# A Fourier-mixing and Hardswish kernel on one core: which batches the first four chunks of a pair take, and when the second batch is loaded

## The chip, the cores and the metric

The kernel runs on one core of a Trainium2 chip. The metric is device time in microseconds (us) of one execution. Before the change, three executions took 1940.53, 1941.27 and 1941.79 us: the median is 1941.27 us.

## What is computed

```python
x: (8, 3008, 256)                                  # 8 batches, float32
X = np.fft.fft(np.fft.fft(x, axis=1), axis=2).real # Fourier mixing, real part
h = X.reshape(24064, 256) @ w_in                   # 256 -> 2048
g = h * np.clip(h + 3.0, 0.0, 6.0) / 6.0           # Hardswish
out = g @ w_out                                    # 2048 -> 256
```

## The kernel before

The sequence length is 3008 = 47 x 64: a row number is n1 * 64 + n2 with n1 below 47 (`N1`) and n2 below 64 (`N2`). The transform over the sequence is done as a 47-point stage (**stage1**) and a 64-point stage (**stage2**), and symmetries of a real input are used: n2 is folded onto 32 values, and so is the last axis.

The eight batches are worked through as four **pairs** of two batches. For a pair, x comes in as 8 pieces of four n2 values each (`NXC` pieces of `XC`). For each piece there is a straight load (`load_forward`) and a gather of the mirrored rows (`load_partners`, an indirect DMA whose row numbers are in `IX`). `fold` adds and subtracts the two (L187 to L201, 5 vector operations a piece, a few more for the last one), stage1 multiplies the result by a table of 47-point sines and cosines, the results are copied to SBUF (tile `z`) and written to a scratch area in DRAM (`zd`). From there `load_g` reads them back in another order, a **group** `gr` of four k1 values at a time for both batches (six groups), stage2 multiplies them by the tables `T`, and the result is the tile `q` that the dense part uses. One row of it is spread over all partitions as `qn` (`spread`, through DRAM; `spread_by_pe` does the same with matmuls).

The dense part takes 12 **chunks** of a pair (`ck`), two from each group, and each chunk in 8 **steps** (`fc`, one step for 256 of the 2048 columns of the hidden layer), so 96 steps a pair and 384 in all; step s below counts from the first one of the program. In a step TensorE makes the two first products u and v (`mlp1_products`, L394), VectorE and ScalarE make the Hardswish of them (`activate`: L403, L413, L415, L440, L443), GpSimd makes sums of the results (`combine`, L457), and TensorE multiplies by seven prepared mixtures of w_out blocks (`mlp2`, L487; in the first chunk the plain blocks, `mlp2_first`, L467). The program is written out by hand: the order on each engine's queue is the order of the source. `mlp1` runs two steps ahead of `mlp2`. Work for later groups and the next pair is put beside given steps by `beside`, ahead of the step's own work or (`at=behind`) after its `mlp1`. When a chunk has ended, `store` transposes its results and sends them out, 8 DMAs of 32 KB from SP's queue in the second step of the next chunk and 8 in the third; `finish` (GpSimd) comes before them in the first.

Before step 0 there is a **prologue**. For the first pair it does not use `stage1` but `stage1_first` (L253): both batches lie side by side on 94 partitions, one table `F0` holds both, and a product is one matmul over the whole. Eight times, in `ORDER` (the last piece first), the prologue loads a piece on GpSimd's queue, folds it on VectorE and makes its stage1. Three pieces are asked for ahead, since their tiles are three. The parts of `zd` that group 0 needs are written at once, the rest by DMAs kept in the list `later`, which steps 1 and 3 issue. Then follow `load_g` of group 0, half of its stage2, and `u` and `v` of steps 0 and 1; the second half of group 0's stage2 stands between these two.

Beside this the weights are prepared (their values are taken apart into exponent and mantissa and put together again): `load_w` brings 16 pieces of 512 KB; `exponent_a` (ScalarE, L604), `exponent_b` (TensorE, L621), `exponent_c` (ScalarE, L624), `mantissa` (VectorE, L632, L633) and `join` (VectorE, L641, L647) treat one; and for w_in `fold_w_in` multiplies it by the cosine table (L673), copies it to `W1` (L675) and moves one row of it into the columns `WN` (L679, SP's queue), which L403 needs. `load_w(0)` to `load_w(3)` are issued late in the prologue, `load_w(4)` to `(7)` once group 0 has arrived (`see`), the others in steps 0 and 1. The calls in steps 0 to 7 are in `first_steps` and `second_steps`. `mix_w_out` (GpSimd, four operations) makes the mixtures for `mlp2`: twice in step 5, and in steps 8 and 9.

Of the kernel before, what the change touches and what calls it, by code (L numbers as in the profile page):

```python
# [58 lines left out]
def kernel(  # L59
# [21 lines left out]
    PR0, PZ0 = 2 * N1, 2 * PZ  # L81
    XC = 4
    NS = N2 // 2
    NXC = NS // XC
    KC = 4
# [29 lines left out]
    F = consts.tile([P, 5 * PB], F32, name="F")  # L115
    F0 = apool.tile([PR0 + 2, 6 * PZ0], F32, tag="a", name="F0")
# [10 lines left out]
    class Pair:  # L127
        def __init__(self, p):
            self.p = p
            self.x, self.xr, self.y, self.z = {}, {}, {}, {}  # L130
            self.zd = self.zq = None
            self.g, self.q, self.qn = {}, {}, {}

    ORDER = [NXC - 1] + list(range(NXC - 1))

    def x_tile(pr, c):
        pool, tag = (spool, "t") if pr.p == 0 and ORDER.index(c) % 3 == 2 else (xpool, "x")
        return pool.tile([PX, XC, D], F32, tag=tag, name="xt")  # L140
# [8 lines left out]
    def load_forward(pr, c):  # L149
        xt = x_tile(pr, c)  # L150
        n = XC if c < NXC - 1 else XC - 1
        if pr.p == 0:
            o = xt[0:PR0 + 2]
            nc.gpsimd.dma_start(out=o[:, 0:n, :], in_=x_pn[0:PR0 + 2, c * XC + 1:c * XC + 1 + n, :])
            if n < XC:
                nc.gpsimd.dma_start(out=o[:, n:XC, :], in_=x_pn[0:PR0 + 2, 0:1, :])
        for b in range(2) if pr.p > 0 else ():
# [12 lines left out]
    def load_partners(pr, c):  # L170
        xr = x_tile(pr, c)
        pr.xr[c] = xr
        i = pr.p * NXC + c
        nr = PX if pr.p > 0 else PR0 + 2
        nc.gpsimd.indirect_dma_start(  # L175
            out=xr[0:nr].rearrange("p n d -> p (n d)"), out_offset=None, in_=x_r,
            in_offset=bass.IndirectOffsetOnAxis(ap=IX[0:nr, i:i + 1], axis=0),
        )

    def fold(pr, c, part, eng):  # L180
        nr = PX - 1 if pr.p > 0 else PR0
# [71 lines left out]
    def stage1_first(pr, c):  # L253
        y = pr.y.pop(c)
        n = XC if c < NXC - 1 else XC - 1

        def table0(i):
            return F0[0:PR0, i * PZ0:(i + 1) * PZ0]

        pt = ps_h.tile([P, 2 * TB], F32, tag="uv", name="pt")[0:PZ0]  # L260
        nc.tensor.matmul(pt[:, 0:n], table0(5), y[:, 0:n, P], start=True, stop=True)
        for k in range(2 if n < XC else 0):
            nc.tensor.matmul(pt[:, n:XC], table0(k + 1), y[:, n + k, P:P + 1], start=(k == 0), stop=(k == 1))

        k = ORDER.index(c)
        pool, tag = (zpool, "z") if k < 2 else (cpool, "c") if k < 5 else (qpool, "q") if k < 7 else (apool, "a")
        z = pool.tile([PZ0, XC, D + 1], F32, tag=tag, name="z")
        nc.scalar.copy(z[:, :, D], pt[:, 0:XC])
        for i in range(XC // 2):
            ps = bank([P, 2, D], "ps1")[0:PZ0]  # L270
            if (c, i) == (NXC - 1, XC // 2 - 1):
                nc.tensor.matmul(ps[:, 0], table0(0), y[:, 2 * i], start=True, stop=False, skip_group_check=True)
                for k, (j, cs) in enumerate([(XC - 1, slice(0, P + 1)), (XC, slice(0, P + 1)),
                                             (XC - 1, slice(P + 1, D)), (XC, slice(P + 1, D))]):
                    nc.tensor.matmul(ps[:, 1, cs], table0(k + 1), y[:, j, cs], start=False, stop=(k % 2 == 1),
                                     skip_group_check=True)
            else:
                nc.tensor.matmul(ps, table0(0), y[:, 2 * i:2 * i + 2, :], start=True, stop=True)
            nc.scalar.copy(z[:, 2 * i:2 * i + 2, 0:D], ps)
        if pr.zd is None:  # L280
            pr.zd = dpool.tile([NG, 2, 2 * KK, 2, NS, D + 1], F32, tag="zd0", name="zd")
        zd = pr.zd[:].rearrange("g b k c n d -> (g b k c) n d")[:, c * XC:(c + 1) * XC, :]

        n0 = PZ0 // NG
        nc.sync.dma_start(out=zd[0:n0], in_=z[0:n0])
        later.append((zd[n0:], z[n0:]))
# [18 lines left out]
    def load_g(pr, gr):  # L305
        g = gpool.tile([P, 2 * KK, D + 1], F32, tag="g", name="g")
        gb = [g[b * N2:(b + 1) * N2] for b in range(2)]
        for b in range(2):
            zd = pr.zd[b, gr] if pr.p > 0 else pr.zd[gr, b]
            zd = zd.rearrange("k c n d -> (c n) k d")  # L310
            if pr.p > 0 or gr > 0:
                nc.sync.dma_start(out=gb[b][:, :, 0:D if pr.p > 0 else D + 1], in_=zd)

        for h in range(2 if pr.p + gr == 0 else 0):
            ks = slice(h * KK, (h + 1) * KK)
            for b in range(2):

                (nc.sync if h + b == 0 else nc.gpsimd).dma_start(
                    out=gb[b][:, ks], in_=pr.zd[gr, b, ks].rearrange("k c n d -> (c n) k d"))
        for b in range(2) if pr.p > 0 else ():  # L320
            nc.sync.dma_start(out=gb[b][:, :, D], in_=pr.zq[gr, :, :, :, b].rearrange("k c n -> (c n) k"))
        pr.g[gr] = g

# [19 lines left out]
    def spread_by_pe(pr, gr, i, ps, copy=nc.scalar.copy):  # L343
        if i == 0:
            pr.qn[gr] = qpool.tile([P, 2 * TB], F32, tag="qn", name="qn")
        for u in range(2):
            kk = 2 * i + u
            nc.tensor.matmul(ps[:, u * P:(u + 1) * P], pr.g[gr][:, kk, D:D + 1].to_broadcast([P, P]),
                             T[:, :, gr, 1, kk], start=True, stop=True)
        copy(pr.qn[gr][:, i * TB:(i + 1) * TB], ps)  # L350
        if i == 1:
            del pr.g[gr]

    def spread(pr, gr):
        pr.qn[gr] = qpool.tile([P, 2 * TB], F32, tag="qn", name="qn")
# [6 lines left out]
    class Chunk:  # L362
# [3 lines left out]
        def __init__(self, pr, ck):  # L366
# [9 lines left out]
            self.blocks = [[(2 * (j % 2) + h, (k1[j], N1 - k1[j])[m]) for j in range(KC) for h in range(2)]  # L376
# [319 lines left out]
    nc.sync.dma_start(out=FI[:], in_=c_stage1[:, 5 * PB + 6 * PZ0:])  # L696
    nc.sync.dma_start(out=F0[:], in_=c_stage1[0:PR0 + 2, 5 * PB:5 * PB + 6 * PZ0])
# [35 lines left out]
    for c in ORDER[0:3]:  # L733
        load_x(first, c)
# [4 lines left out]
    for k, c in enumerate(ORDER):  # L739
        for part in range(2):  # L740
            fold(first, c, part, nc.vector)
        if k == NXC - 1:

            exponent_a(0)
        stage1_first(first, c)
        if k < NXC - 1:
            keep_awake(1)
        if k + 3 < NXC:
            load_x(first, ORDER[k + 3])
        else:  # L750
            for j in (2, 3) if k == 5 else ():
                load_w(j)
        if k == 4:
            load_w(0)
            load_w(1)
            load_t(0, slice(0, KK))
        elif k == 1:
            nc.sync.dma_start(out=C[:], in_=dim)
    load_g(first, 0)
    load_t(0, slice(KK, 2 * KK))  # L760

    seen = wpool.tile([P, 1], F32, tag="seen", name="seen")
    see(first.g[0][:, 0, 0:1])
# [23 lines left out]
    stage2(first, 0, 0)  # L787
    spread_by_pe(first, 0, 0, bank([P, TB], "ps3")[:])
# [7 lines left out]
    def beside(p):  # L796
# [7 lines left out]
        late = 4 if p == 0 else 0  # L804
        if p == 0:
            put(5, load_g, cur, 1)
            for gr in range(1, NG):
                put(gr + 1, load_t, gr)
            put(NF - 1, close_w)
            put(NF - 1, nc.sync.dma_start, F[:], c_stage1[:, 0:5 * PB])  # L810
# [6 lines left out]
        for gr in range(1, NG):  # L817
# [32 lines left out]
    stage2(first, 0, 1, copy=nc.vector.tensor_copy)  # L850
    spread_by_pe(first, 0, 1, spare[0][:, 0], copy=nc.vector.tensor_copy)
# [62 lines left out]
    for s, (p, ck, fc) in enumerate(steps):  # L914
# [4 lines left out]
        if s < NF:  # L919
# [6 lines left out]
            if s == 5:  # L926
                see(chunk(s + 1)[0].a[s + 1][:, 0, 0, 0:1])
                mix_w_out(0)
                mix_w_out(1)
        else:  # L930
# [6 lines left out]
            if s < NF + 2:  # L937
                mix_w_out(s - NF + 2)
# [11 lines left out]
def _tables(B, S, D):  # L950
# [19 lines left out]
    f1 = np.zeros((2, 64, 5, 64))  # L970
    f1[:, :N1, :, :2 * NK1] = f[:5].reshape(5, N1, -1).swapaxes(0, 1)

    f0 = np.zeros((128, 6, NK1 // 4, 2, 8))
    for b in range(2):
        f0[b * N1:(b + 1) * N1, :, :, b] = f.reshape(6, N1, NK1 // 4, 8).swapaxes(0, 1)

# [3 lines left out]
    for i in range(B):  # L980
        n = i % 2 * (64 if i > 1 else N1)
        row[n:n + N1, i // 2] = ((i * N1 + np.arange(N1)[::-1, None]) * 2 + 2) * npc - 1 - np.arange(npc)
    sign = 1.0 - 2.0 * (np.arange(128)[:, None] % 2)
    f = np.concatenate([f1.reshape(128, -1), f0.reshape(128, -1), row.reshape(128, -1), sign], axis=1)
# [45 lines left out]
```

## Time and profile before

| | |
|---|---|
| span of the profiled execution | 1938.6 us |
| median of the times | 1941.27 us, that is 2.7 us more than that span |
| busy share of the span | TensorE (PE) 99%, VectorE (DVE) 74%, ScalarE (ACT) 35%, GpSimd (POOL) 73% |
| granted TensorE clock | full in all 40 slices |
| first fold on VectorE starts | 7.88 us |
| first dense product (L394) starts | 43.60 us |
| first product with the mixtures (L487, step 8) starts | 110.87 us |
| DMA share in 0 to 25, 25 to 50, 50 to 75, 75 to 100 us | 0.87, 0.81, 0.68, 0.47 |

How to read it: the page gives one profiled execution, with busy times by engine, and then the chain of work that ended last. The trace behind it can be asked for the instructions of a stretch in order of time (the timeline), and for busy times in given stretches (the windows). A name like `u<-q,W` says what is written from what; L394 is the line of the program; SPq and POOLq are the queues on which SP and GpSimd issue DMAs, and a DMA's time there is that of its issue, not of its transfer. In a timeline row the first number is the start, the second the time from there to the end of the last instruction merged into the row, and `[0.52 <-DMA WN<-W]` tells how long the engine sat idle before it and what ended that. TensorE makes a float32 product in two passes, so one matmul of the program is counted as x2.

### The profile page before, as it was taken

Reading aid. Unit: us, or ns where it says so; the run is one execution under the profiler, and the core shown is the slowest. Engines: PE = TensorE matmul, PEld = TensorE weight load, DVE = VectorE, ACT = ScalarE, POOL = GpSimd, SP = SyncE. Lnnn points to the kernel's source line nnn. Section 1 sums busy time; section 2 is a strip of 40 time slices with the busy share of each in tenths; the row PEclk is TensorE's granted clock in tenths of the full one; section 3 lists DMA queues with packets and bytes.
Section 4 is the critical chain, followed back from the end, with each engine's and each line's share of the span. In section 5 each row is a group of like instructions: output and inputs, shape, how many; then the busy total and the mean of one; then the engine's idle time right before and its main releaser. Section 6 shows DMA issues by size and latency. Waiting matters only on the chain.

```text
span 1938.6 us, 27871 instructions
## 1 busy us (share of the span) xinstructions
PE 1922.3 (99%) x9220; PEld 1654.3 (85%) x9220; DVE 1438.2 (74%) x2780; ACT 679.9 (35%) x1161; POOL 1418.2 (73%) x1624
## 2 busy tenths in 40 slices
PE   9999999999999999999999999999999999999997
PEld 4688888888988888888898888888899888888887
DVE  7877777767777777777787777777778777777777
ACT  5634333333333333333333333333333333333332
POOL 4088888887678877787678877878666667666664
PEclk9999999999999999999999999999999999999999
DMA  8522221211112222121111221222110101101000
GB/s 248 177 60 63 59 53 50 55 46 33 35 34 58 67 56 55 44 52 33 34 36 49 53 55 44 52 53 50 35 28 20 28 17 28 34 11 28 21 18 20
DMA packets 149998, 96.57 MB, mean 50 GB/s; under 512 B 118991, under 2 KB 132307, under 8 KB 149854
## 3 DMA queue, kind: packets, MB, share of 16 engines
q1 hardware_dynamic: 138378, 57.57, 12.4%
q0 software_dynamic: 10816, 37.07, 6.7%
q8 instruction: 72, 1.18, 0.3%
q14 instruction: 72, 0.59, 0.1%
q10 hardware_dynamic: 660, 0.16, 0.0%
HBM read 57.44 MB, written 37.32 MB: 49 GB/s over the span
## 4 chain that ended last, share of the span: by engine, by line
PE 95%; DVE 2%; DMA 1%; issue 1%; ACT 1%; POOL 0%; SPq 0%; DVEq 0%; ACTq 0%; POOLq 0%
PE acc L487 56%; PE v L394 16%; PE u L394 16%; PE ps L337 2%; PE acc L467 1%; PE ps L223 1%; DVE a L443 1%; DMA xt<-in_x_dram,IX 1%; PE spare L673 1%; DVE s L403 0%; ACT t L440 0%; DVE o L548 0%; DVE u L424 0%; PE ex L621 0%; POOL xt L175 0%
## 5 line engine op out<-in xcount | busy, mean ns | idle before, releaser
L457 POOL TENSOR_TENSOR c<-a 128x512 f32<-128x512 f32 (+1 forms) x375 | 468.8, 1250 | 362.8 <-PE acc L487 312.4
L487 PE MATMUL acc<-c,G 128*128 128x256 f32 (+1 forms) x3008 | 696.9, 374 | 0.0
L440 ACT ACTIVATE t<-u,half 128x512 f32<-128x512 f32 (+1 forms) x384 | 260.6, 679 | 1141.9 <-DVE u L413 1058.9
L487 PEld LDWEIGHTS acc<-c,G 128*128 128x128 f32 x3008 | 565.4, 190 | 71.1
L403 DVE SCALAR_TENSOR_TENSOR s<-qn,WN,u 128x256 f32<-128x256 f32 (+1 forms) x768 | 330.6, 472 | 334.3 <-PE u L394 333.2
L487 PE MATMUL acc<-a,G 128*128 128x256 f32 (+1 forms) x2256 | 541.3, 375 | 0.0
L487 PEld LDWEIGHTS acc<-a,G 128*128 128x128 f32 x2256 | 421.5, 190 | 71.1 <-issue 17.5
L394 PE MATMUL v<-q,W 127*128 127x256 f32 (+1 forms) x1536 | 389.3, 375 | 3.0 <-DVE a L443 3.0
L394 PE MATMUL u<-q,W 128*128 128x256 f32 (+1 forms) x1536 | 388.0, 375 | 0.9 <-ACT q L340 0.9
L443 DVE SCALAR_TENSOR_TENSOR a<-t,u 128x512 f32<-128x512 f32 (+2 forms) x448 | 264.0, 601 | 102.3 <-ACT t L440 98.8
L394 PEld LDWEIGHTS v<-q,W 127*128 127x128 f32 x1536 | 287.8, 190 | 43.9 <-DVE a L443 3.6
L394 PEld LDWEIGHTS u<-q,W 128*128 128x128 f32 x1536 | 285.7, 190 | 37.6 <-issue 1.9
L457 POOL TENSOR_TENSOR c<-a,c 128x256 f32<-128x256 f32 (+1 forms) x375 | 268.6, 716 | 29.4
L457 POOL TENSOR_TENSOR c<-c,a 128x256 f32<-128x256 f32 (+1 forms) x375 | 268.5, 716 | 29.4
L413 DVE TENSOR_TENSOR u<-s,v 128x512 f32<-128x512 f32 x352 | 245.0, 696 | 36.7
L443 DVE SCALAR_TENSOR_TENSOR a<-t,v 128x512 f32<-128x512 f32 (+1 forms) x480 | 263.6, 566 | 0.3 <-ACT t L440 0.2
L440 ACT ACTIVATE t<-v,half 128x512 f32<-128x512 f32 (+1 forms) x384 | 260.5, 678 | 0.4 <-PE acc L487 0.2
L415 DVE TENSOR_TENSOR v<-v,s 128x512 f32<-128x512 f32 x352 | 243.9, 693 | 0.0
L457 POOL TENSOR_TENSOR r<-w,e 128x256 f32<-128x256 f32 (+1 forms) x92 | 88.7, 985 | 3.6
L497 ACT ACTIVATE e<-acc 128x512 f32<-128x512 f32 (+2 forms) x184 | 83.4, 544 | 0.0
L548 DVE STREAM_TRANSPOSE o<-r 128x256 f32<-128x256 f32 (+1 forms) x192 | 72.5, 415 | 0.2
L457 POOL TENSOR_TENSOR w<-w,e 128x512 f32<-128x512 f32 (+1 forms) x46 | 57.5, 1249 | 3.6
(110 smaller groups left out, 770.9 us busy)
## 6 DMA issues: line engine op xcount, KB each, us to landing
out_dram<-o SPq DMA_DIRECT2D x747, 32.0 KB
zd<-z SPq DMA_DIRECT2D x48, 192.0 KB
g<-zd SPq DMA_DIRECT2D x36, 256.0 KB
xt<-in_x_dram POOLq DMA_DIRECT2D x21, 256.0 KB
qn<-qd SPq DMA_DIRECT2D x19, 256.0 KB
st<-in_moe_w_in_dram POOLq DMA_DIRECT2D x8, 512.0 KB
st<-in_moe_w_out_dram POOLq DMA_DIRECT2D x8, 512.0 KB
xt<-in_x_dram POOLq DMA_DIRECT2D x17, 192.0 KB
```

What stands on the lines that cost most here:

```text
L223: nc.tensor.matmul(ps[b][h * PB:(h + 1) * PB, 0:n], F[rows(b), 0:PB], y[rows(b), 2 * h:2 * h + n], start=True, stop=not last, skip_group_c ...
L337: nc.tensor.matmul(ps[:, blk, u * P:n].rearrange("p (b k) -> p b k", b=2), g[:, kk, blk * (P + 1):blk * (P + 1) + P], T[:, :, gr, blk, kk, ...
L394: nc.tensor.matmul(ps[:, i, 0:nq], W1[r, blk, f * P:(f + 1) * P], q[r, blk, of:of + nq], start=True, stop=True)
L403: nc.vector.scalar_tensor_tensor(s[:, i, 0:nq], qn[:, of:of + nq], WN[:, f:f + 1], u[:, i, 0:nq], op0=AL.mult, op1=AL.add)
L413: nc.vector.tensor_tensor(u[:], s[:], v[:], op=AL.add)
L415: nc.vector.tensor_tensor(v[:], v[:], s[:], op=AL.subtract)
L440: nc.scalar.activation(t, h, AF.Relu, bias=half[:], scale=scale)
L443: nc.vector.scalar_tensor_tensor(dst, t, 1.0, h, op0=AL.min, op1=AL.mult)
L457: (eng or nc.gpsimd).tensor_tensor(out, in0, in1, op=AL.add)
L487: nc.tensor.matmul(ch.acc[i // 2][:, i % 2, 0:ch.n], G[:, i, fc, :], mv, start=(fc == 0 and i % 2 == 0), stop=(fc == NF - 1), skip_group_c ...
L497: nc.scalar.mul(ch.e[:, k:i + 1, 0:ch.n], ch.acc[i // 2][:, 0:i + 1 - k, 0:ch.n], 1.0 / WS)
L548: nc.vector.transpose(o[:, 0:n // DH, h], ch.r[:, m, h, 0:n].rearrange("p (j i) -> p j i", i=DH))
```

## The change

The first pair's first two groups are no longer made for both batches at once. Chunks 0 and 1 take 8 values of k1 from **batch 0**, chunks 2 and 3 the same values from **batch 1**; from chunk 4 on all is as before. So the prologue needs the x of batch 0 alone. A `Half` stands for one batch: its 8 pieces are taken as four double pieces m, piece m on partitions 0 to 46 and piece m + 4 on partitions 64 to 110 (`load_half`, `fold_half`, `stage1_half`), and the matmuls of the two halves use rows and columns 0 to 63 and 64 to 127 of TensorE. The tables `F0` are gone, `F` has a sixth table and is loaded at the start.

In the prologue the straight loads of batch 0 go on SP's queue, the gathers on GpSimd's; all four double pieces have tiles of their own, and `load_w(0)` to `(3)` come right behind them. Stage2 of group 0 is one call (`stage2_half`, two k1 values in the place of the second batch). The x of batch 1 is loaded in steps 2, 4, 4 and 5, folded on GpSimd in steps 3, 5, 6 and 7, and goes through `stage1_half` in steps 5, 7, 8 and 9. `mix_w_out` is moved to steps 4, 6, 9 and 11, and its `see` is dropped. Pair 1's loads start at step 12 and come every 8 steps (before: step 8, every 8). The diff, cut:

```diff
-    ORDER = [NXC - 1] + list(range(NXC - 1))
+    ORDER = [NM - 1] + list(range(NM - 1))
...
+    def load_half(hb, m, queue, pool=xpool, tag="x"):
+        hb.x[m], hb.xr[m] = x_tile(pool, tag), x_tile(pool, tag)
+        for h in range(2):
+            c = m + h * NM
+            nr = N1 + 1 if h else PB
+            n = XC if c < NXC - 1 else XC - 1
+            rows, o = x_pn[hb.b * N1:hb.b * N1 + nr], hb.x[m][h * PB:h * PB + nr]
+            queue.dma_start(out=o[:, 0:n, :], in_=rows[:, c * XC + 1:c * XC + 1 + n, :])
+            if n < XC:
+                queue.dma_start(out=o[:, n:XC, :], in_=rows[:, 0:1, :])
+        gather(hb.xr[m], hb.b * NM + m)
...
+    def stage1_half(hb, m):
+        y = hb.y.pop(m)
...
+        pt = ps_h.tile(...) if starting[0] else bank([P, 2 * TB], "pt")
+        for h in range(2):
...
+            nc.tensor.matmul(o[:, 0:n], table(5, h), y[rows(h), 0:n, P], start=True, stop=True)
...
+        nc.scalar.copy(z[:, :, D], pt[0:PX, 0:XC])
+        for i in range(XC // 2):
+            ps = bank([P, 2, D], "ps1") if starting[0] or i else ps_h.tile([P, 2, D], F32, tag="uv", name="ps1")
+            for h in range(2):
+                o = ps[h * PB:(h + 1) * PB]
...
+                nc.tensor.matmul(o[:, 0:n], table(0, h), y[rows(h), 2 * i:2 * i + n], start=True, stop=not end,
+                                 skip_group_check=True)
...
+            nc.scalar.copy(z[:, 2 * i:2 * i + 2, 0:D], ps[0:PX])
...
+        n0 = 2 * 4 * KK if hb.b == 0 else PZ
+        for h in range(2):
...
+            nc.sync.dma_start(out=dst[0:n0], in_=src[0:n0])
+            if n0 < PZ:
+                later.append((dst[n0:], src[n0:]))
...
+    def load_g_half(hb, gr, queue=nc.sync):
...
+        for t in range(2):
+            (queue if t else nc.sync).dma_start(out=g[t * N2:(t + 1) * N2, 0:KK], in_=zd[t])
...
+            if pr.p == 0 and ck < 4:
+                k1 = [ck % 2 * KC + j + 1 for j in range(KC)]
+                b = [ck // 2] * KC
...
-    for c in ORDER[0:3]:
-        load_x(first, c)
+    hb = halves[0]
+    for k, m in enumerate(ORDER):
+        load_half(hb, m, nc.sync, *((xpool, "x"), (xpool, "x"), (spool, "t"), (apool, "a"))[k])
+        if k == 0:
+            nc.sync.dma_start(out=F[:], in_=c_stage1[:, 0:6 * PB])
...
+    for j in range(4):
+        load_w(j)
+    nc.sync.dma_start(out=C[:], in_=dim)
+    load_t(0)
+    for k, m in enumerate(ORDER):
         for part in range(2):
-            fold(first, c, part, nc.vector)
+            fold_half(hb, m, part, nc.vector)
...
-        stage1_first(first, c)
+        stage1_half(hb, m)
...
-    stage2(first, 0, 0)
-    spread_by_pe(first, 0, 0, bank([P, TB], "ps3")[:])
+    stage2_half(hb, 0)
+    spread_by_pe(hb, 0, bank([P, TB], "ps3")[:])
...
+            put(3, load_g_half, halves[0], 1)
+            put(4, stage2_half, halves[0], 1)
+            put(5, spread_half, halves[0], 1)
...
+            hb = halves[1]
+            for k, m in enumerate(ORDER):
+                put((2, 4, 4, 5)[k], load_half, hb, m, nc.sync, *((qpool, "q") if k < 2 else (xpool, "x")))
+                for part in range(2):
+                    put((3, 5, 6, 7)[k], fold_half, hb, m, part, nc.gpsimd)
+                put((5, 7, 8, 9)[k], stage1_half, hb, m)
+            put(4, mix_w_out, 0)
+            put(6, mix_w_out, 1)
+            put(9, mix_w_out, 2)
+            put(11, mix_w_out, 3)
+            put(11, load_g_half, hb, 0)
+            put(11, load_g_half, hb, 1)
+            for gr in range(2):
+                put(12 + 4 * gr, stage2_half, hb, gr)
+                put(13 + 4 * gr, spread_half, hb, gr)
...
-                put(NST * (gr - 2) + 12, load_g, cur, gr)
-            s2(NST * (gr - 1) + (late if gr == 1 else 0), cur, gr)
+                put(NST * (gr - 2) + (12 if p > 0 or gr > 2 else 17), load_g, cur, gr)
+            s2(NST * (gr - 1), cur, gr)
...
-                t = 2 * late + (9 - late // 4) * c
+                t = 9 * c if p > 0 else 12 + 8 * c
...
-    stage2(first, 0, 1, copy=nc.vector.tensor_copy)
-    spread_by_pe(first, 0, 1, spare[0][:, 0], copy=nc.vector.tensor_copy)
```

More of the change, by code (lines that the diff above doesn't have):

```diff
@@ L149, in load_forward @@
     def load_forward(pr, c):
-        xt = x_tile(pr, c)
+        xt = x_tile()
         n = XC if c < NXC - 1 else XC - 1
[L152 to L157, printed above, removed]
+        for b in range(2):
             i = 2 * pr.p + b
@@ L308, in load_g @@
         for b in range(2):
[L309 to L319, printed above, removed]
+            zd = pr.zd[b, gr] if pr.p > 0 else pr.zd[b][gr]
+            nc.sync.dma_start(out=gb[b][:, :, 0:D if pr.p > 0 else D + 1], in_=zd.rearrange("k c n d -> (c n) k d"))
         for b in range(2) if pr.p > 0 else ():
@@ L695 @@
     keep_awake(9)
[L696 to L697 removed]
+    nc.sync.dma_start(out=FI[:], in_=c_stage1[:, 6 * PB:])
     bias = wpool.tile([P, 2], F32, tag="bias", name="bias")
@@ L968, in _tables @@
     f[2:5:2] = f[2:5:2, ::-1]
[L970 to L975, printed above, removed]
+    f1 = np.zeros((2, 64, 6, 64))
+    f1[:, :N1, :, :2 * NK1] = f.reshape(6, N1, -1).swapaxes(0, 1)
     npc = N2 // 8
```

193 lines of the change are left out of this document (111 added, 82 removed).

## The prediction

> **What bounds the kernel now.** I read the engines' busy times first, then the windows, then the timeline of the start, and last the places after step 8 that the change touches.
>
> ```profile
> PE 1922.3 (99%) x9220; PEld 1654.3 (85%) x9220; DVE 1438.2 (74%) x2780; ACT 679.9 (35%) x1161; POOL 1418.2 (73%) x1624
> ...
> 75.00:100.00 25.00, 25.00 (x88) 15.64 (x87) 20.47 (x39) 14.66 (x24) 3.06 (x6) 1.00 0.47 122
> ```
>
> TensorE (PE) is the bound. In the chain that ended last its pieces follow each other without a gap from 66.44 us to the end, so from there a matmul added is time added, and a wait of PE is time lost. What can be won lies ahead of 48.7 us, where PE mostly multiplies zeros to stay awake:
>
> ```profile
> 7.88 0.55 DVE L187 TENSOR_TENSOR xt<-xt 94x381 f32<-94x381 f32 x1 [3.53 <-DMA xt<-in_x_dram,IX]
> ...
> 29.73 0.68 DVE L187 TENSOR_TENSOR xt<-xt 94x508 f32<-94x508 f32 x1 [0.40 <-DMA xt<-in_x_dram,IX]
> ...
> 32.31 0.17 DVE L195 TENSOR_TENSOR y<-xt 94x8 f32<-94x8 f32 x1
> ...
> 43.60 1.13 PE L394 MATMUL u<-q,W 128*128 128x256 f32 x4 [0.95 <-ACT q L340]
> ...
> 45.84 0.48 DVE L403 SCALAR_TENSOR_TENSOR s<-qn,WN,u 128x256 f32<-128x256 f32 x1 [0.52 <-DMA WN<-W]
> ```
>
> Eight folds run from 7.88 to 32.48, some waiting for x. The second L403 at 45.84, 13.36 us after the last fold, waits for WN: the first weights are prepared behind the last stage1, and that chain ends last (group 0 itself let u start at 43.60).
>
> **Part by part.**
>
> *Earlier start.* Folds on VectorE (DVE) take 2.60 us from start to start (20.08 to 22.67, plus the last 0.08); the first took 7.88 to 10.91 and gets two more sums (the 94x127 rows are 0.21 apart) and two small ones: 3.6. Four folds end at 7.9 + 3.6 + 3 x 2.6 + 0.2 = 19.5 if x keeps up. Batch 0 is 4 x 224 rows of 4 KB = 3.67 MB; at the 280 GB/s that the DMA view shows for this stretch it takes 13 us and, begun at 2.5 with 0.2 MB of F, is there at 16.3. The last fold wants it at 16.7. `load_w(0)` is issued behind four gathers (1.25 us apart from 2.8, so at about 8.6) and lands about 19; its first use was 0.4 ahead of the last fold's end. So 32.48 becomes 19.5, less 0.3 for the last stage1 in half arrays: **-12.7**. Bounds: -14 if the first x comes 1 us earlier, -11 if x and weights together move at the window's mean of 244 GB/s (3.87 MB then 18.4, and the weights behind it). The group chain ran 0.5 us ahead of the weights and keeps that: two DMAs more on SP (0.6 us each) against two fewer on POOL.
>
> *Stage1 of batch 1 in the dense part.* Four `stage1_half` are now PE time. The nearest row is stage1 of later pairs:
>
> ```profile
> 148.92 1.03 PE L394 MATMUL v<-q,W 127*128 127x256 f32 x4
> ...
> 149.88 1.09 PE L223 MATMUL ps<-y,F 47*64 47x512 f32 x8
> ...
> 150.89 1.56 PE L487 MATMUL acc<-a,G 128*128 128x256 f32 x6
> ...
> 152.29 1.89 PE L487 MATMUL acc<-c,G 128*128 128x256 f32 x8
> ```
>
> From v to acc<-c are 3.37 us; without stage1 (119.51 to 121.67) 2.16. So eight passes of 512 columns cost 1.21 where a pass alone takes 0.43 (L467, four in 1.72): four quarters of the array work at once, two passes each (0.86) plus 0.35. `stage1_half` has eight such passes, but h goes with its own rows and its own columns: two quarters, four passes each, 1.71 + 0.35, and 0.2 for the four-column products: 2.25. The first one has in its busier quarter 0.43 less and eight passes of 128 columns (0.11 each) more, and short products: 2.8. Sum 3 x 2.25 + 2.8 = **+9.5**. Bounds: 7.3 with no overhead; 16.6 if the two quarters do not overlap (eight passes in a row, 4.0, and 4.6 for the first). The Trainium skill (TensorE: Matmul & The Clock Gate, Part 2) says that matmuls stay in program order and only weight loads are pulled ahead. Taken strictly, two passes of one quarter behind each other would hold up the other quarter, and a `stage1_half` would cost 0.43 more; by the row above, which would then take over 2.1, this does not happen.
>
> *Stage2.* Calls behind the first dense product in the open: before two (101.03 and 123.40, 0.89 each by the chain), after three (steps 4, 12, 16); the one removed at 45.43 lay in a wait. **+0.9**.
>
> *A new wait at step 12.* `load_g_half` of batch 1 stands in step 11, behind the 16 stores of steps 9 and 10 on SP's queue; stage2 of it opens step 12.
>
> ```profile
> 113.89 1.03 PE L394 MATMUL u<-q,W 128*128 128x256 f32 x4
> ...
> 118.65 0.76 DVE L548 STREAM_TRANSPOSE o<-r 128x256 f32<-128x256 f32 x2
> ...
> 119.56 10.00 SPq L554 DMA_DIRECT2D out_dram<-o  x16
> ```
>
> Count from u of step 9's `mlp1` (113.89 here). The stores end 15.67 us later, two loads are issued by 17.0 and land by 18.4 (in the prologue g was there 1.3 after the last issue). PE reaches step 12 after three steps of 4.76, at 14.3. PE, with mlp1 of step 14 queued behind, waits **+4.1** (3 to 5.5 with landing times of 0.3 to 2.8; the two loads for group 1 come behind and are needed only in step 16).
>
> *Hidden, or nearly.* Batch 1's folds on POOL take 7 us (first) and 5.1 (L187 to L195: 1.26, 1.09, 1.26, 1.26, 0.22); POOL works 3.06 of 25 us in this stretch, and the last ends some 8 us ahead of its use. x loads on SP stand ahead of WN columns in steps 2 and 4; by the order of issue they leave 3 us of room. Group 1 of batch 0 is loaded one step ahead, with 1 us of room. Copies of z: 1.3 us of ACT each. Pair 1's folds now fall into the steps next to `finish`. Pair 1 has just that once before:
>
> ```profile
> 751.48 1.89 PE L487 MATMUL acc<-c,G 128*128 128x256 f32 x8
> 751.63 0.73 POOL L457 TENSOR_TENSOR c<-a,c 128x256 f32<-128x256 f32 x1
> ```
>
> POOL's last sum ends at 752.36, and PE reads it six passes of 0.215 after 751.48, at 752.78. No stall, but only 0.4 us of cover; each of eight such places would cost what exceeds it. The moved mixing is ready steps ahead. For all these I take **+0.5**, of 0 to 5.
>
> Sum: -12.7 + 9.5 + 0.9 + 4.1 + 0.5 = **+2.3 us** on the span of 1938.6. The median lies 2.7 above that span: 1941.27 + 2.3 = **1943.6**. 0.2% (3.9 us) is about what a measurement of this kernel can tell from no change; this is inside it.
>
> **Rivals.**
>
> 1. *The wait at step 12 does not appear*: loads issued faster than 0.6 us each, or PE late there anyway. Against it stands the row of 16 stores. Without the 4.1: 1939.5. Chance 0.18.
> 2. *The start gains more*: x through two queues comes sooner, the first fold starts 1 us earlier (-14), and neither the wait nor the 0.5 counts, stage1 at 8.5: -14 + 8.5 + 0.9 = -4.6, 1936.7. For it: DMA slices above 300 GB/s occur. Chance 0.10.
> 3. *Quarters do not overlap* (slower): stage1 costs 16.6, and the last stage1 ahead of the dense part 1.7 more: -11.0 + 16.6 + 0.9 + 4.1 + 0.5 = +11.1, 1952.4. It decides the sign from some 11 us on. Against it stands the L223 row. Chance 0.08.
> 4. *Folds on POOL slow the weights on VectorE* (slower). In steps 3 and 5, `mantissa` of pieces 10 to 15 (L632 0.42, L633 0.69, twelve instructions) meets the folds. If each waits for half a POOL instruction (0.63), step 3 gets 5.0 us longer on DVE and step 5 2.5; PE has 1.0 us until `v` waits for the gate, and 0.9 from the stage2 put there. About +4 on top: 1947.6. No row of before shows POOL and these instructions side by side; L403 and L443 keep 0.47 and 0.6 beside POOL. The Trainium skill (GPSIMD Engine Reference, Key points) says that GpSimd shares its SBUF interfaces with VectorE, with contention for two SBUF inputs (L633) or a two-port mode: that speaks for this rival. Chance 0.19.
> 5. The change does what it says: the order of instructions shows batch 0's loads alone ahead of the dense products.
>
> **From cases to numbers.** My forecast (1941 to 1946) has 0.45. Faster by over 0.2%: rival 2 and a bit of 1, 0.13. Slower: 3, 4 and the forecast's upper end, 0.35. Within: 0.52. The range takes in rival 1, the ends of the start and of the wait, and rival 4 with a bad stage1, and leaves out 2 and 3: 1938 to 1950.
>
> **What would show it.** In the changed profile: the last prologue fold at 19 to 20 us; the first L394 product near 31 and the WN wait ending near 33; the step from mlp1 to mlp2 with a `stage1_half` 2.2 us longer than one without; PE idle about 4 us in front of the first stage2 of batch 1, released by the DMA of g; the first product with mixtures at 110.87 - 12.7 + 7.3 (three `stage1_half`), near 105.5. I am wrong if there is no such wait, if PE idles in steps 3 to 9, or if the folds in the prologue still wait for x.

## The result, and the profile after

The changed kernel is slower: 1962.01 us in the median of 4 executions (1960.84 to 1963.99), the kernel before 1940.9 (1940.38 to 1941.79, 4 executions) beside it. The ratio is 1.0109, 95% interval [1.0095, 1.0123]. The prediction was 1943.6, range 1938 to 1950. The profiled execution has a span of 1960.5 us, 21.9 more than before.

The page's engine line, and the windows row of the stretch that had no gap before (columns: stretch, its length, busy time of PE, PEld, DVE, ACT and POOL, granted clock, DMA share, GB/s):

```profile
PE 1930.0 (98%) x9268; PEld 1657.2 (85%) x9268; DVE 1430.5 (73%) x2761; ACT 681.0 (35%) x1162; POOL 1433.8 (73%) x1639
...
75.00:100.00 25.00, 23.18 (x91) 14.74 (x92) 15.28 (x22) 9.65 (x18) 21.72 (x28) 0.86 0.55 144
```

PE is busy 7.7 us longer than before, but the span grew by 21.9: the larger part is PE waiting, and a granted clock of 0.86 where it was 1.00. The view of PE's waits in the changed kernel names the first of them (sum, how often, longest):

```profile
PE ps L382 <- DMA g<-zd: 11.2, 3, 7.2
PE v L470 <- DVE a L519: 4.3, 6, 2.5
```

L382 is stage2 of a half, and it waited for its group three times. In the timeline of the start (L203 and L211 are the folds now, L470 the dense products, L479 the sum that needs WN):

```profile
10.26 0.56 DVE L203 TENSOR_TENSOR xt<-xt 111x381 f32<-111x381 f32 x1 [5.85 <-DMA xt<-in_x_dram,IX]
...
15.82 0.69 DVE L203 TENSOR_TENSOR xt<-xt 111x508 f32<-111x508 f32 x1 [2.01 <-DMA xt<-in_x_dram,IX]
...
24.77 0.17 DVE L211 TENSOR_TENSOR y<-xt 111x8 f32<-111x8 f32 x1
...
36.28 1.13 PE L470 MATMUL u<-q,W 128*128 128x256 f32 x4 [0.41 <-ACT q L385]
...
38.79 0.48 DVE L479 SCALAR_TENSOR_TENSOR s<-qn,WN,u 128x256 f32<-128x256 f32 x1 [0.37 <-DMA WN<-W]
```

The folds wait for x and end at 24.94 (32.48 before), not at 19.5. The timelines at steps 4 and 12 show what stood in no term, or in a small one:

```profile
73.13 1.27 SPq L366 DMA_DIRECT2D g<-zd  x2
...
76.82 2.05 PE L382 MATMUL ps<-T,g 128*128 128x128 f32 x8 [3.58 <-DMA g<-zd]
...
78.66 3.62 PE L543 MATMUL acc<-a,G 128*128 128x512 f32 x4
```

```profile
130.08 9.53 SPq L630 DMA_DIRECT2D out_dram<-o  x16
...
138.25 1.12 POOL L159 DMA_DIRECT2D xt<-in_x_dram  x2
...
139.68 0.99 POOL L170 DMA_INDIRECT xt<-in_x_dram,IX  x1 [0.30 <-issue]
139.71 2.60 SPq L366 DMA_DIRECT2D g<-zd  x4
...
146.14 2.04 PE L382 MATMUL ps<-T,g 128*128 128x128 f32 x8 [7.23 <-DMA g<-zd]
...
147.97 1.91 PE L470 MATMUL u<-q,W 128*128 128x256 f32 x4
```

Read the second numbers: behind each wait the same products take twice as long (L382 2.05 and 2.04 for 1.05, L543 3.62 for 1.88, L470 1.91 for 1.03). The windows row 145 to 150 gives the granted clock for it, and the one before it the full engines that the loads of g met:

```profile
140.00:145.00 5.00, 0.00 (x0) 0.00 (x0) 0.00 (x0) 0.00 (x0) 3.40 (x4) 0.89 0.96 264
145.00:150.00 5.00, 3.86 (x13) 3.54 (x14) 0.07 (x1) 0.59 (x1) 0.00 (x0) 0.50 0.12 28
```

**Where the 21.9 us came from.** For each step I took the start of its u product in the changed kernel's timeline less that in the kernel before. The difference is the time lost or won up to there; where it jumps, something happened. One line for each profiled execution, one execution of each kernel (the experiments are below; "span" is the difference of the spans):

```
                         step 0   4      5      12     13     15    span
changed kernel            -7.3   -5.5   +1.9  +10.6   +9.7  +20.3  +21.9
e1_load_g_step10          +0.2   +1.7   +8.1  +16.8  +15.9  +16.9  +18.5
e2_x_step13               -3.8   -1.9   +4.4  +13.1  +12.2  +19.1  +20.8
e3_awake_step12           -1.1   -0.8   +6.8  +15.5  +14.6  +23.1  +24.7
e4_load_g_step1           +1.5   +4.1   +6.0  +14.7  +13.8  +23.8  +25.2
e5_awake_start            -7.3   -5.3   +1.1   +9.8   +8.9  +18.9  +20.5
e6_x_on_pool              -7.1   -6.8   -0.6   +8.1   +7.2  +17.0  +18.7
e7_waits_mended           -7.2   -7.5   -6.3   +2.4   +1.5   +2.4   +3.9
e8_waits_and_x            -8.3   -8.0   -6.8   +1.9   +1.0   +2.0   +3.5
e9_stage1_twice           -7.8   -8.1   -6.9   +8.6   +7.8   +8.6  +10.1
e10_tables_behind         -8.1   -7.8   -6.6   +2.0   +1.1   +2.1   +3.8
e11_tables_behind_nine    -9.2   -8.7   -7.5   +1.2   +0.3   +1.2   +2.9
e12_waits_mended_nine     +0.2   +1.9   +3.8  +12.5  +11.6  +12.5  +13.9
```

In the changed kernel: -7.3 at the start; +1.8 in steps 0 to 2; +7.5 in step 4, of which 0.9 is stage2 itself; +8.7 from step 5 to 12, that is 9.55 for the four `stage1_half`, less the 0.89 of a stage2 that the kernel before had in this stretch; +9.7 around step 12; +1.6 from there to the end (one more stage2, 0.9, and 0.7 of small things).

### The profile page after: what moved, and what is told of

The parts are those of the page before. It is cut to its first block, busy times and chain, and to the rows that moved or that the text cites. A ratio compares the mean times of both kernels' runs of the same rounds, so it can differ in the third digit from the quotient of the medians.

```text
span 1960.5 us, 27996 instructions
## 1 busy us (share of the span) xinstructions
PE 1930.0 (98%) x9268; PEld 1657.2 (85%) x9268; DVE 1430.5 (73%) x2761; ACT 681.0 (35%) x1162; POOL 1433.8 (73%) x1639
## 4 chain that ended last, share of the span: by engine, by line
PE 93%; DVE 3%; DMA 1%; ACT 1%; issue 1%; SPq 1%; POOL 0%; DVEq 0%; ACTq 0%
PE acc L563 55%; PE v L470 16%; PE u L470 16%; PE ps L412 2%; PE ps L264 1%; PE acc L543 1%; DVE a L519 1%; DMA xt<-in_x_dram,IX 1%; DVE s L479 1%; ACT t L516 1%; PE ps L317 0%; SPq L630 0%; DMA g<-zd 0%; DVE o L624 0%; PE spare L749 0%
## 5 line engine op out<-in xcount | busy, mean ns | idle before, releaser
L563 PE MATMUL acc<-c,G 128*128 128x256 f32 (+1 forms) x3008 | 697.3, 375 | 0.3 <-POOL c L533 0.2
L563 PEld LDWEIGHTS acc<-c,G 128*128 128x128 f32 x3008 | 565.2, 190 | 72.1 <-POOL c L533 1.1
L479 DVE SCALAR_TENSOR_TENSOR s<-qn,WN,u 128x256 f32<-128x256 f32 (+1 forms) x768 | 330.2, 471 | 350.2 <-PE u L470 347.9
L563 PE MATMUL acc<-a,G 128*128 128x256 f32 (+1 forms) x2256 | 541.4, 376 | 0.0
L563 PEld LDWEIGHTS acc<-a,G 128*128 128x128 f32 x2256 | 422.2, 190 | 70.5 <-issue 17.6
L470 PE MATMUL v<-q,W 127*128 127x256 f32 (+1 forms) x1536 | 390.9, 376 | 4.3 <-DVE a L519 4.3
L470 PE MATMUL u<-q,W 128*128 128x256 f32 (+1 forms) x1536 | 389.2, 376 | 0.4 <-ACT q L385 0.4
L470 PEld LDWEIGHTS v<-q,W 127*128 127x128 f32 x1536 | 289.2, 190 | 45.2 <-DVE a L519 4.7
L470 PEld LDWEIGHTS u<-q,W 128*128 128x128 f32 x1536 | 286.1, 190 | 39.1 <-issue 4.3
```

What stands on the lines that cost most here:

```text
L470: nc.tensor.matmul(ps[:, i, 0:nq], W1[r, blk, f * P:(f + 1) * P], q[r, blk, of:of + nq], start=True, stop=True)
L479: nc.vector.scalar_tensor_tensor(s[:, i, 0:nq], qn[:, of:of + nq], WN[:, f:f + 1], u[:, i, 0:nq], op0=AL.mult, op1=AL.add)
L563: nc.tensor.matmul(ch.acc[i // 2][:, i % 2, 0:ch.n], G[:, i, fc, :], mv, start=(fc == 0 and i % 2 == 0), stop=(fc == NF - 1), skip_group_c ...
```

## The experiments

My theory after this reading: the terms are separate, and the large ones that the prediction missed are two late loads of g, each made dearer by the clock that PE lost while it waited. The rivals were that a wait mended only shows the next one, and that the half clock has to do with something other than the wait.

**e1, e2, e3, e4: one wait at a time.** Each run changes the changed kernel in one place:

```diff
e1   -put(11, load_g_half, hb, 0)           +put(10, load_g_half, hb, 0)      (and group 1 alike)
e2   -put(t, load_x, nx, c)                 +put(t + (p + c == 0), load_x, nx, c)
e3   +put(12, keep_awake, 8, C[:].rearrange("p h d -> p (h d)"))   ahead of stage2_half
e4   -put(3, load_g_half, halves[0], 1)     +put(1, load_g_half, halves[0], 1)
```

> Theory: the changed kernel loses 9.7 us at step 12 (TensorE waits 7.2 us for g of batch 1, then runs some 2.4 us late at half the granted clock), because the loads of g are issued behind all 16 stores of steps 9 and 10. Here both loads of g for batch 1 are called in step 10, behind only the 8 stores of step 9. They should be issued about 5 us sooner, near 135 us instead of 139.7, and land before TensorE wants them at 138.9: no wait, clock full, 9 to 10 us less than the changed kernel, near 1952.5. Rival: g takes 5 us to land wherever it stands (141.0 to 146.1 in the changed kernel): then it lands near 141.5, some 2.5 us of wait stay and most of the clock loss goes, near 1955.

> Only pair 1's first load of x is moved, from step 12 to step 13, so that it is not under way beside g of batch 1. Theory: g lands late since 0.9 MB of x, asked for at 138.3 to 140.7 us, share the DMA engines with it. Then g lands some 1.5 us after its issue has ended at 141.0, as in the prologue, the wait at step 12 falls from 7.2 to about 3.7 us, as the prediction had it (4.1), and the clock drops less or not at all: 3.5 to 6 us less, 1956 to 1958.5. Rival: the landing is long for another reason (the stores ahead in the same queue): wait still about 7 us, time unchanged at 1962.

> Eight products of 512 columns (C by ones, results not used, 0.86 us each) are put in front of the first stage2 of batch 1 in step 12, where TensorE waits. Theory: the half clock after the wait comes from TensorE's idleness. Then the wait for g stays (the filler ends at about 145.8, g is there at 146.1), but what follows runs at full clock: 2 to 2.4 us less than the changed kernel, near 1959.7. Rival: the clock drop has nothing to do with the idle time, or the filler delays what follows: unchanged or up to 1 us more.

> The load of g of batch 0, group 1, is called in step 1 instead of step 3. Theory: it was issued at 73.1 us, just when TensorE wanted it (73.2), and cost 3.6 us of wait and some 3.0 us of half clock. Called in step 1 it is issued near 56 us, behind the WN columns of step 0, and is there long before: 6 to 7 us less than the changed kernel, near 1955.5. Rival: it is the transfer of x of batch 1 or another load that holds up step 4, and the wait only changes its name: less than 2 us gained.

Measured: e1 1955.61 us, ratio to before 1.0073 [1.0048, 1.0098]; e2 1957.89, 1.0085 [1.0068, 1.0102]; e3 1960.85, 1.0101 [1.0084, 1.0118]; e4 1961.88, 1.0097 [1.0078, 1.0115]. By the table each did at its own place what the theory of two late loads said: in e1 the jump from step 13 to 15 fell from 10.6 to 1.0, in e4 the jump from step 4 to 5 from 7.5 to 1.9. In e2, with pair 1's first x a step later, the same loads of g were issued behind the same 16 stores and landed sooner:

```profile
142.18 2.60 SPq L366 DMA_DIRECT2D g<-zd  x4
...
144.34 1.13 POOL L159 DMA_DIRECT2D xt<-in_x_dram  x2
...
145.78 0.99 POOL L170 DMA_INDIRECT xt<-in_x_dram,IX  x1 [0.30 <-issue]
...
145.87 2.04 PE L382 MATMUL ps<-T,g 128*128 128x128 f32 x8 [4.47 <-DMA g<-zd]
```

The wait is 4.47, close to the 4.1 of the prediction; the rest up to 7.23 was the neighbour on the engines. The loss from step 12 to 15 fell from 9.7 to 6.1. In e3 eight products of no use filled the wait:

```profile
143.66 7.03 PE L766 MATMUL awake<-C,ones 128*128 128x512 f32 x16
151.20 1.13 PE L382 MATMUL ps<-T,g 128*128 128x128 f32 x8 [0.51 <-DMA g<-zd]
152.16 1.03 PE L470 MATMUL u<-q,W 128*128 128x256 f32 x4
```

L382 and u are back at 1.13 and 1.03: the half clock came from PE's idleness and not from what it waited for. The loss from step 12 to 15 fell from 9.7 to 7.6; in the median of the times (1960.85 against 1962.01, with ranges that overlap) this gain isn't clear of noise.

The total times followed only in part. The median of e2 lies in its expected range, and two executions of e1 (1952.20 and 1952.36, mean granted clock 0.997 and 0.996) stand where its expectation had them, while the other two (1958.86 and 1961.20) have 0.991; the median of e4 stayed 6 us above its expectation, and only its fastest execution (1955.69) is at it. The first column of the table says why: in the profiled executions, which are the slowest of their run in e2, e3 and e4, the start, which none of the four touches, stood 3.5 to 8.8 us later than in the changed kernel's profile. In e1's timeline of PE:

```profile
1.68 9.89 PE L766 MATMUL awake<-Z,ones 128*128 128x512 f32 x18 [1.68 <-DVE half L776]
13.02 0.28 PE L303 MATMUL pt<-y,F 47*64 47x4 f32 x4 [1.45 <-DVE y L213]
...
18.85 3.66 PE L317 MATMUL ps<-y,F 47*64 47x512 f32 x8
```

The nine products that keep the clock up end at 11.6, the first y comes 1.45 us later, and then stage 1 takes 3.66 where it takes 1.94. That was not in my theory, nor in the prediction.

**e5 and e6: the start.** e5 has twelve such products; e6 also puts the straight rows on POOL's queue, each pair ahead of the gather of the same piece, to see why the folds wait.

```diff
e5   -    keep_awake(9)
     +    keep_awake(12)
e6   as e5, and
     -        load_half(hb, m, nc.sync, *((xpool, "x"), ...)[k])
     +        load_half(hb, m, nc.gpsimd, *((xpool, "x"), ...)[k])
```

> Twelve products that keep the clock up at the start, not nine; nothing else. In the four runs so far the first u product stood at 43.8, 39.8, 42.5 and 45.1 us, in the profile of the changed kernel at 36.3, with the same program up to there. Theory (clock): in the four, PE was idle for 1.45 to 2.14 us ahead of the first stage 1 product (0.72 in the changed kernel's profile) and the granted clock was 0.50 to 0.58 from 15 to 30 us (1.00 in the changed kernel's); three more products cover the gap, so clock 1.00 from 15 us on, first u product at 36 to 37.5, time 1960 to 1961.5, and its runs lie within 1.5 us of each other. Rival (transfers): the start varies because the gathered rows land at different times; then the first u product stands anywhere from 36 to 45 again and the time scatters by several us as before.

> As e5, and the straight rows of the first batch go out on POOL's queue, each pair ahead of the gather of the same step, and not on SP's queue. Theory (sharing): the gathers are late because SP's queue, which has all the straight rows, F, C and T at hand, takes half of the engines from them; with one queue in the order of use the last fold ends near 20 us (24.94 in the changed kernel's profile), the first u product stands at 31.5 to 33, and the time is some 4 to 5 us under e5: 1956 to 1957. Rival (the gather's own rate, or its issue): the gathered rows need their time whatever is beside them, and POOL issues them later by the 8 issues of about 0.6 us put ahead of them; then the last fold ends at 25 us or later, the first u product stands at 36 to 40, and the time is 1960 to 1964.

Measured: e5 1961.02 us (1958.81 to 1963.29), ratio 1.0099 [1.0081, 1.0117]; e6 1962.75 (1959.04 to 1963.15), 1.0108 [1.0090, 1.0126]. In e5 the first u stood at 36.30, as the clock theory said, but the executions still lay 4.5 us apart, not 1.5: that part of the expectation fell, and e12 below prices the start without the other waits. In e6 the folds came no earlier (last fold's end 25.47, 24.96 in e5; first u 36.51): the rival came out, the sharing of the engines by two queues isn't what makes the rows late, and the theory of e6 is dropped.

**e7 and e8: all waits at once.** e7 is e5 with e1's and e4's lines and with two products by C between u and v of step 1; e8 is e7 with e6's line.

```diff
     def mlp1_products(ch, fc, awake=0):
...
         for blk, ps in ((0, u), (1, v)):
+            if blk and awake:
+                keep_awake(awake, C[:].rearrange("p h d -> p (h d)"), bank([P, 2 * TB], "awake"))
...
-    uv = mlp1_products(*chunk(1))
+    uv = mlp1_products(*chunk(1), awake=2)
```

> As e5, with three waits mended at once: group 1 of batch 0 loaded at step 1 and not 3, both groups of batch 1 loaded at step 10 and not 11, and two products that keep the clock up ahead of the v product of step 1. Theory (the budget of the changed kernel's trace is a sum of separate terms): 6.6 off at step 4, 9.7 off at step 12, 1.5 off at steps 0 to 2, so 1960.8 - 17.8 = 1943 us, the time before within 0.2%: what stays is the earlier start of 7.3 us against 9.4 us of stage 1. Rival (something behind the waits is due at the same time): a wait mended shows the next one, and half of it or more comes back: 1950 us or more.

> As e7 with the straight rows on POOL's queue as in e6. Theory (sharing, and separate terms): 4 to 5 us under e7, 1938 to 1939 us, about 2 us under the kernel before. Rival (the gather's own rate): not under e7, 1943 us or more.

Measured: e7 1944.30 us (1943.66 to 1945.69, 10 executions), ratio 1.0015 [1.0005, 1.0025]; e8 1945.05 (1943.86 to 1945.59), 1.0020 [1.0010, 1.0029]. The sum of the separate terms was right to 1.3 us, and no wait of that size came up in their place; PE's waits and the same window in e7:

```profile
PE v L472 <- DVE a L521: 2.1, 6, 1.1
...
PE ps L382 <- DMA g<-zd: 0.7, 1, 0.7
```

```profile
75.00:100.00 25.00, 25.00 (x106) 14.93 (x105) 16.13 (x28) 11.96 (x22) 22.23 (x30) 1.00 0.63 163
```

So some 17 of the 21 us were waits, and clock lost behind them, that a few lines of the source take away, and what is left, 3.1 us (1944.30 - 1941.22), is the trade itself: 7.2 won at the start against stage 1 and stage2. That e7 comes near the 1943.6 of the prediction is chance: its start wins 5.5 us less than forecast, and the wait at step 12 is gone. e8 gains nothing that can be measured, as e6.

**e9: is stage 1 paid in full?** As e7, each wide product of batch 1's `stage1_half` made twice.

```diff
-            for h in range(2):
+            for h in (0, 1) * (1 + hb.b):
                 o = ps[h * PB:(h + 1) * PB]
```

> As e7, and each wide product of the four stage1_half calls of batch 1 is made twice (the second run writes the same sums again). Theory (those four calls stand on TensorE's path at their full length, which is the larger part of what e7 still loses): by their rows in the changed kernel's trace the second run adds about 2.4 us in the first call and 1.9 us in each of the other three, 8.0 us in all, so e7 + 8.0, near 1952 us. Rival (PE waits at these steps anyway, for activate or for the gates, and part of stage 1 lies in that wait): e7 + 4 us or less.

Measured: 1951.74 us (1950.39 to 1952.01), ratio 1.0058 [1.0043, 1.0073]; e7 + 7.4 in the medians, + 8.4 with the kernel before beside each taken off, + 6.2 between the two profiled spans. The same call in e7 (first row) and in e9 (second fence), timeline of PE:

```profile
97.84 1.91 PE L317 MATMUL ps<-y,F 47*64 47x512 f32 x8
```

```profile
99.36 3.63 PE L317 MATMUL ps<-y,F 47*64 47x512 f32 x16
```

Eight passes more cost 1.72, the four passes of 0.43 of one quarter: two quarters run side by side, and in this call all of it is on the path. The rival (half of it hidden, + 4 or less) falls. Of the 1.91, 0.2 is paid once, and the second run was worth about the 8.0 expected.

**e10, e11, e12: what the rows of x wait for, and the price of the start.** e10 is e8 with C and the first T behind the weights on POOL's queue (0.52 MB). e11 is e10 with nine products at the start again. e12 is e7 with nine.

```diff
e10  -    nc.sync.dma_start(out=C[:], in_=dim)
     -    load_t(0)
     +    nc.gpsimd.dma_start(out=C[:], in_=dim)
     +    load_t(0, queue=nc.gpsimd)
e11  as e10, with keep_awake(9)
e12  as e7, with keep_awake(9)
```

> As e8, and C and the first T (0.52 MB) go out on POOL's queue behind the first four weight pieces, not on SP's queue beside the rows of x. Theory (bytes): up to 20 us the engines are full (share 1.01 to 1.06) and move 240 to 258 GB/s in e8 whatever the queue; the last fold waits for all that is ahead of it in bytes, so 0.52 MB less is 2.1 us: last fold's end near 22 us (24.26 in e8), the first u product near 33.2 (35.32), time 1943 us, 2 us under e8 and within 0.2% of the kernel before. Rival (what follows the fold is due at the same time, the weights' chain and the tables): the folds come earlier and the first u product does not, 1945 us.

> As e10 with nine products at the start again, not twelve. In e10 the last fold ended 1.4 us earlier than in e8 and the first u product did not come earlier: PE worked without a gap from 14.8 us to 27, because the twelve products lasted to 14.8 while the first y stood from 11.7. Theory (the twelve products, needed to hold the clock where the first rows come at 10 to 11 us, are what is late once they come at 8.4): nine end near 11.3 us, the last stage 1 of batch 0 starts behind the last fold at 22.8 and not at 24.7, the first u product stands near 33.7 us (35.5 in e10), time 1942.2 us, within 0.2% of the kernel before. Rival (the chain of the weights behind the fold, or the clock): the first u product stays at 35 us or later, 1944 us.

> As e7 with nine products at the start, as in the changed kernel: the price of the unsteady start by itself, with the later waits gone that could swallow it. Theory (clock): some executions start as in the changed kernel's profile (first u product at 36.3), others 3.5 to 8.8 us later with the granted clock near 0.5 from 15 to 30 us; the runs spread from 1944 to 1953 us, median 1946 to 1951. Rival (a later start is swallowed by waits further on, or the start is as steady as in e7): 1944 to 1945 us with a spread of 2 us.

Measured: e10 1943.93 us (1942.91 to 1945.09), ratio 1.0016 [1.0007, 1.0025]; e11 1943.11 (1941.41 to 1952.45, 12 executions), 1.0017 [1.0006, 1.0028]; e12 1947.73 (1943.57 to 1954.24, 8 executions), 1.0034 [1.0022, 1.0045]. In e10 the last fold ended at 22.82 (24.26 in e8), in e11 at 23.42. The other eleven profiled executions of changed kernels have 23.92 to 25.90, so with fewer bytes ahead the rows do come earlier; by how much, one execution each can't say (2.1 us were expected). In e10 the rival came out for the first u: it did not move (35.51), since PE had no gap from the twelve products to the end of stage 1. In e11 it moved to 34.38, short of the 33.7 expected, and with nine products two of the twelve executions (1950.58 and 1952.45) are again some 8 us longer. None of the three has a median below the kernel before. e12 shows the unsteady start alone, as its theory had it: its executions lie 10.7 us apart (2.0 in e7), and the median is 3.4 us over e7. The time goes with the clock: the mean granted clock is 0.999 in the fastest execution, 0.996 in that of 1949.06 us and 0.993 in the slowest. Its windows against e5's (twelve products, second fence):

```profile
15.00:20.00 5.00, 5.00 (x18) 2.51 (x17) 4.21 (x8) 1.14 (x3) 0.00 (x0) 0.50 1.03 274
...
30.00:35.00 5.00, 5.00 (x15) 1.16 (x15) 0.00 (x0) 1.80 (x5) 0.00 (x0) 0.50 0.15 26
```

```profile
15.00:20.00 5.00, 4.27 (x28) 2.17 (x24) 3.13 (x6) 1.64 (x4) 0.00 (x0) 1.00 1.03 243
```

## Why the prediction was wrong, step by step

| term | on record | in the profile | |
|---|---|---|---|
| earlier start | -12.7 (-14 to -11) | -7.3, then +1.8 in steps 0 to 2 | mis-sized |
| stage1 of batch 1 | +9.5 | +9.5 | right |
| stage2 | +0.9 | +0.9 | right |
| wait at step 12 | +4.1 (3 to 5.5) | +9.7 | right mechanism, mis-sized |
| others | +0.5 (0 to 5) | +6.6 at step 4, +0.7 | wrong |

The forecast was +2.3 and the span grew by 21.9. Of the 19.6 us between them 7.2 lie in the start, 6.8 in the others and 5.6 in the wait at step 12. Stage 1 is right in its sum; its four calls cost 2.85, 2.06, 2.48 and 1.95 us, for a forecast of 2.8 and three times 2.25.

- **Earlier start: "if x keeps up" failed.** The 280 GB/s was the step. The windows from 2 to 22 us show what the DMA engines moved in the changed kernel, nearly full:

```profile
2.00:22.00 20.00, 17.51 (x58) 7.44 (x57) 10.17 (x25) 8.59 (x10) 5.71 (x7) 1.00 0.99 233
```

  At 233 GB/s that is 4.66 MB in 20 us; batch 0 and F are 3.87 MB, so 0.8 MB of C, T, weights and the first z went along with them. The same window of the kernel before moved 261 GB/s at a DMA share of 0.94, so 280 was no mean there either. The last gather was there before 22.19, not at 16.3, and the folds waited 8.9 us in all: the first began 2.4 us later than forecast, and two later waits took 3.0. I had bounded the rate by the stretch's mean of 244 but let nothing else share it, and C and T, whose issue the change moved to the start, were in no sum. e10 and e11 speak for the bytes, and e6 against the queue, by one execution each. A small slip besides: 20.08 to 22.67 plus 0.08 is 2.67 us a fold and not 2.60. From the last fold's end to the first u it is 11.3 us, 11.1 before: that part held. The 1.8 after it is a place that I called free ("the one removed at 45.43 lay in a wait"): that stage2 had filled PE's wait for v, and without it PE idled 2.48 us and the clock fell to 0.66. The clock is most of it: from step 0 to 2 the changed kernel lost 1.9 us, and e6, which waited 2.60 there with its clock at 1.00, lost 0.4.

- **Others: "Group 1 of batch 0 is loaded one step ahead, with 1 us of room" failed.** SP issued it at 73.13 to 74.40, behind columns of WN (from 68.36) and two loads of T (from 71.84), and PE wanted it at 73.2. The working of the 1 us is not on record; I had set the stage2 of step 4 behind u of `mlp1(5)` at 81.19 in the kernel before, but a step's `ahead` work comes before the step's own, right behind `mlp1(4)` at 76.88. One step wrong in the program order made 1 us of room out of a lack of 3.6. e4 settles it: loaded two steps earlier, the stage2 runs without a wait, and the difference from step 4 to 5 falls from 7.5 to 1.9, 0.9 of it stage2 itself. With this wait PE idled in steps 3 to 9, which the prediction had named, like folds that wait for x, as a sign of being wrong.

- **The wait at step 12** came, behind the 16 stores as told (9.53 us of issue). The two loads of its group were the first of the four issued from 139.71 to 142.31, and g was there at 146.14, where the prediction took 1.3 us from the last issue to the landing. Two things were left out: pair 1's x, which the change itself had moved to step 12, shared the engines (7.23 of wait against 4.47 in e2), and the half clock after it (about 2.4; e3).

- **The half clock was in no term.** It cost about 3 us at step 4, 2.4 at step 12 and some 1.5 in step 1. At the start it cost the profiled execution of the changed kernel nothing (1.00 there), and the median of e12 3.4 over e7. The Trainium skill (TensorE: Matmul & The Clock Gate, Part 1) says that PE's clock falls to half after an idle window of about 3.4 us and comes back after as long a busy one. At step 12 the runs agree (0.50 after a wait of 7.23, and L563 at its full 1.46 again 5 us behind it). At the start they do not: in five executions the clock fell after a gap of 1.45 to 2.14 us, in eight with a gap of 0.72, 0.48 or none it did not, and the half clock lasted for some 10 us and more of busy PE. The measurement decides; before a wait of 1.5 us or more is called cheap, its clock has to be priced.

- **Rivals.** 1 (no wait at step 12) and 2 (a better start) fell. 3 fell: eight passes in 1.91. 4: the mechanism was there at no price, but it met less than the prediction counted: the first fold on POOL waited for x until 71.87, when the eight instructions of step 3 were done but for one (71.63, at its usual 0.69). In step 5, beside folds and a gather on POOL:

```profile
88.45 1.05 DVE L708 TENSOR_SCALAR top<-st 128x512 int32<-128x512 int32 x1
...
89.54 1.64 DVE L709 SCALAR_TENSOR_TENSOR top<-st,top 128x512 f32<-128x512 uint32 x1
...
91.95 3.00 DVE L708 TENSOR_SCALAR top<-st 128x512 int32<-128x512 int32 x1
```

  Alone they take 0.42 and 0.69. The Trainium skill (GPSIMD Engine Reference, Key points) names two SBUF inputs as a case of contention, and L709 agrees with it (1.64 for 0.69 once); L708, which slowed most, has one input, and no run here shows why. But from step 5 to 6 the difference grew by 2.85 in the changed kernel and in e7 alike, which stage 1 (2.6 to 2.7 by its rows) nearly fills: VectorE had the room. 5 holds, and the sums on POOL near `finish` cost PE 0.2 us once. The first product with mixtures, forecast at 105.5 us, came at 119.29 (110.87 before).

## What to carry to other kernels

A wait of the bounding engine costs its length and the clock that is lost in it; where a wait can't be taken away, products of no use in it can keep the clock (e3: the products behind it at 1.03 for 1.91; e7 against e12: 3.4 us of the median). When loads move, list every transfer that shares those microseconds, those of other queues and those moved for tidiness as well, and divide all their bytes by the measured rate. For every load that a late step needs, compare the time of issue with the time of use in the same frame and in program order; here two loads, one or two steps late, and the clock lost behind them were 16 of the 18 us that made a trade of 3 us into a loss of 21.

## What was not expected of the hardware

- The same prologue, run in the changed kernel and in e1 to e4, brought the first u at 36.3 to 45.1 us. With nine products at the start, PE's gap ahead of the first stage 1 was 0.72 us (clock kept at 1.00) in the changed kernel and 0.48 in e11, and 1.45, 2.14, 1.63, 2.14 and 1.62 in e1, e2, e3, e4 and e12 (clock 0.50 to 0.70 in the window 15 to 20). With twelve it was kept in all six profiled executions. Why the gap differs is in the nine products' own time, 9.49 to 10.79 us, and in the landing of the first gather, 9.9 to 11.4 (9.1 in e11). The nine products start slow and then double their pace, at a time that differs: by the starts of their weight loads the passes are 0.86 us apart up to 6.96 us and 0.43 apart from 7.58 on in the changed kernel, and 0.43 apart from 5.00 on in e12. The granted clock of these first microseconds reads 1.00 all the same, so it can't be taken from the windows there. What sets these times stays open.
- The length of a gap alone does not decide: ahead of v in step 1 PE idled 2.48 and 2.62 us with clocks of 0.66 and 0.78 in that window (changed kernel, e5), and 2.60 and 2.58 us with 1.00 (e6, e3).
- At the start the half clock lasted for 10 to 20 us with PE busy without a gap (0.50 from 15 to 35 us in e12), at steps 4 and 12 for about 4 to 6 us. That the products there are on 47 rows or on zeros is a possible reason; it was not tried.
